# A spectral filter with a feed-forward gate on one core: the transform over d handed on from chunk to chunk, two numbers of its planner, and one accumulating load asked for a step sooner

## The chip, the cores and the metric

The kernel runs on one core of a Trainium2 chip. A core has a matrix engine (TensorE, PE in the profile), a vector engine (VectorE, DVE), a scalar engine (ScalarE, ACT), GpSimd (POOL) and SyncE (SP), which here only issues DMAs. PE's weight loads have a row of their own in the profile (PEld). Each engine works through its own queue in order, and engines wait for each other through semaphores. A letter q behind an engine's name (SPq, ACTq) is its sequencer, which issues DMAs.

The metric is the time of one execution on the device in microseconds (us), smaller is better. The kernel before was run three times.

## The reference, cut to what matters

```python
x = A_x                                   # 1 x 2048 x 1024
xn = _layernorm(x, axis=-1)
X = rfft2(xn)                             # over s (2048) and d (1024)
s = irfft2(X * (w_r + 1j * w_i))          # spectral filter
h = silu(xn @ w1)                         # 1024 -> 3584
g = silu(h @ w2)                          # 3584 -> 1024
out = x + s * g
```

So there are two branches on the same normed input: a Fourier filter over both axes, and a feed-forward net whose output gates the filter's. At the end they are multiplied and the input is added.

## The kernel before, in words

**Two matrix products, and everything else between them.** Rows of x are cut in four chunks c of 512 rows, each in four parts p of 128. Fp32 operands are split in two fp16 halves, so that each product is three fp16 matmuls. The first product (`mm1`, lines 457 to 479) walks a list `order` of 112 groups (c, f), one for each chunk and each 128 columns of w1; a group is 24 matmuls (L466). Its silu is taken by ACT (L475) one group later. The second product (`mm2`, lines 545 to 551) is done as seven block products m with eight output tiles j each; a group (m, j) is two times 21 matmuls (L549, L550, L551).

**The planner.** The spectral branch has no place of its own. It is written as Python generators, and the loop over the groups takes steps of them when the program is written. After a group's matmuls come `settle` (the evacuation of the group ahead), `tick` (DMAs that were put off by some groups) and `work` (line 1523). `work` takes one step of the queue `wq` (loading and splitting weights), in seven of eight calls one of `xq` (maxima of the filter and of w2), and then up to three steps of `bg`, in which the spectral branch stands in order. In mm1 that is once a group, in mm2 twice. Whether `bg` may go on is decided by a meter: a callback (line 220) adds up an estimated time for each PE and DVE instruction in `clock["pe"]` and `clock["dve"]`, and `bg` stops while the DVE's clock is more than `LEAD` = 1.0 us ahead of the PE's. The DVE's clock is never let fall more than 1.0 us behind. A step may also yield `PAUSE`, which ends the call; any other yielded value has no effect. An instruction's place in the text so fixes what is queued ahead of it on its engine.

**The transform over d.** `fd_gen(c)` (lines 816 to 915), one generator for each chunk, is the first part of the forward Fourier transform. For part p, `fa_mat(c, p)` (lines 799 to 806) makes 24 matmuls of 128 columns into a PSUM tile `fa`; the tag "ft" has two such tiles. `fa_evac(c, p)` (lines 808 to 814) clears a strip of a tile `L` on POOL (L811) and copies the PSUM tile to it with two ACT instructions (L812, L813). `bfly(p)` (lines 820 to 868) then is DVE work in two steps. The loop of lines 870 to 878 runs over i = 0 to 5: matmuls of part i, evacuation of part i - 1, butterflies of part i - 2. Each pass has at least two yields, also where it has nothing to do. Chunk 0 has its four `fa_mat` and two of its `fa_evac` elsewhere, in the entry of the kernel, and passes 0 and 1 are empty for it.

After the butterflies come four radix-4 steps j (lines 894 to 911): `high_r(j - 1)` on ACT (L884, L886), two DVE instructions, `low_r(j - 1)` (L889, L890), `radix4` on DVE, and a sum `total[j]` (L909, tile `vt`). Line 910 then takes 0.8 us off the DVE's clock. After the four, `high_r(3)` and `low_r(3)` end the chunk.

**What follows in bg.** When the four chunks are through and `w2max_gen` is done, the memory of the forward part is closed, and `f_gen` (the transform over s, the filter, the way back) and the four `i_gen` (c in the order 1, 3, 0, 2; lines 1254 to 1453) follow. An `i_gen` makes its matmuls `iu` (L1280 for odd c, L1288 for even c) into the two PSUM tiles of tag "ft"; they are evacuated by ACT (`uc`, L1294) and DVE (`ub`, L1296, L1297). Ahead of them POOL copies an edge into the input tile `zt` (L1249, L1252).

**wmax_gen** (lines 921 to 943), in `xq`, finds the largest filter value: 18 DVE maxima, one more over them (L935), a reduction over the partitions on POOL (L937), and then on DVE a power of two of that (`pow2`, L230, and lines 940 to 942). One yield stands between POOL's instruction and `pow2`.

**w2_gen** (lines 411 to 453), in `wq`, makes the operands of mm2. Step n loads raw tile n + 4 on SP's queue (L420, tile `jr`, six buffers), splits tile n on ACT (L257, `w<-jr`) and finishes tile n - 1 on DVE (L260). For the products m = 4 and 5 the operand is a sum of two blocks: `join(n + 2)` (L424) has POOL issue a DMA that adds the second block of w2 to raw tile n + 2.

Of the kernel before, what the change touches and what calls it, by code (L numbers as in the profile page):

```python
# [132 lines left out]
def spectral_ffn(ctx, tc, x, w_r, w_i, w1, w2, ca, kc, ci, tw, pm, out):  # L133
# [29 lines left out]
    def small(name, n=1):  # L163
        return sm.tile([128, n], F32, name=name)
# [51 lines left out]
    clock = {"pe": 0.0, "dve": 0.0}  # L216
# [12 lines left out]
    def pow2(e, m):  # L229
        nc.vector.tensor_single_scalar(e.bitcast(I32), m.bitcast(I32), 0x7F800000, op=OP.bitwise_and)  # L230
        nc.vector.tensor_single_scalar(e, e, 2.0**-100, op=OP.max)

    def radix4(sign, b, d, o):

        sub = nc.vector.tensor_tensor
        plus, minus = ((2, 7), (6, 3)) if sign < 0 else ((6, 3), (2, 7))

        def pick(i):
            st = i[1] - i[0]
            stop = i[1] + (1 if st > 0 else -1)  # L240
            return o[:, i[0]:stop:st]

        sw = d[:, 1, ::-1]
        sub(o[:, 0:2], b[:, 0], b[:, 1], op=OP.add)
        sub(o[:, 4:6], b[:, 0], b[:, 1], op=OP.subtract)
        sub(pick(plus), d[:, 0], sw, op=OP.add)
        sub(pick(minus), d[:, 0], sw, op=OP.subtract)
# [8 lines left out]
    def high(hi, raw, scale):  # L256
        nc.scalar.activation(hi, raw, AF.Copy, scale=scale)  # L257

    def low(lo, raw, scale, hi):
        nc.vector.scalar_tensor_tensor(lo, raw, scale, hi, op0=OP.mult, op1=OP.subtract)  # L260
# [146 lines left out]
    def w2_block(m, q, b):  # L407
        r, h = W2_BLOCKS[m][b]
        return w2[(2 * q + r) * 128:(2 * q + r + 1) * 128, h * 512:(h + 1) * 512]

    def w2_gen():

        todo = [(m, q) for m in range(7) for q in range(NP)]
        raw = {}

        def load(n):
            if n < len(todo):
                m, q = todo[n]
                raw[n] = J["p"].tile([128, 512], F32, name=f"jr{n}", tag="jr", bufs=6)
                nc.sync.dma_start(raw[n], ws[m][q] if m in ws else w2_block(m, q, 0))  # L420

        def join(n):
            if n < len(todo) and todo[n][0] in SUMMED:
                nc.gpsimd.dma_start(raw[n], w2_block(*todo[n], 1), accum_op=OP.add)  # L424

        def split(n):
            m, q = todo[n]
            if q % 7 == 0:
                w2t[m, q // 7] = fp.tile([128, 7, 2, 512], F16, name=f"w2_{m}_{q // 7}", tag="big", bufs=4)
            high(w2t[m, q // 7][:, q % 7, 0], raw[n], sc2[:, q:q + 1])  # L430

        def rest(n):
            m, q = todo[n]
            w = w2t[m, q // 7][:, q % 7]
            low(w[:, 1], raw.pop(n), sc2[:, q:q + 1], w[:, 0])
            ready2[0] = n

        for n in range(4):
            load(n)
        yield 0  # L440
        yield 0
        for n, (m, q) in enumerate(todo):
            while q % 7 == 0 and (done2[0] < m - 1 or chunks[0] <= (3 if m else q // 7) and m < 2):
                if n and ready2[0] < n - 1:
                    rest(n - 1)
                yield 0
            load(n + 4)
            join(n + 2)
            split(n)
            if n and ready2[0] < n - 1:  # L450
                rest(n - 1)
            yield 0.1
        rest(n)
# [345 lines left out]
    def fa_mat(c, p):  # L799
        ps = pt.tile([128, 8, 128], F32, name=f"fa{c}_{p}", tag="ft")  # L800
        sl, xt = slice(p * 128, (p + 1) * 128), xnT[c]
        for d in range(8):
            nc.tensor.matmul(ps[:, d], xt[:, 0, d, sl], A["ca"][:, 0, d], start=True, stop=False)
            nc.tensor.matmul(ps[:, d], xt[:, 0, d, sl], A["ca"][:, 1, d], start=False, stop=False)
            nc.tensor.matmul(ps[:, d], xt[:, 1, d, sl], A["ca"][:, 0, d], start=False, stop=True)
        psa[c, p] = ps

    def fa_evac(c, p):
        ps = psa.pop((c, p))
        t0 = A["p"].tile([128, 8, 2, 65], F32, name=f"L0_{c}_{p}", tag="L0", bufs=2)  # L810
        nc.gpsimd.memset(t0[:, :, 1, 0:1], 0.0)  # L811
        nc.scalar.activation(t0[:, :, 0], ps[:, :, 0:65], AF.Copy)  # L812
        nc.scalar.activation(t0[:, :, 1, 1:64], ps[:, :, 65:128], AF.Copy)  # L813
        l0[c, p] = t0

    def fd_gen(c):
# [50 lines left out]
            stt(rv(1, 7), up(qq[:, 3]), -RH, up(pp[:, 3]), op0=OP.mult, op1=OP.subtract)  # L867
            tt(v[:, 1, 0:1], ee[:, 0, 0, 0:1], ee[:, 1, 0, 0:1], op=OP.subtract)

        for i in range(6):  # L870
            if i < 4 and c:
                fa_mat(c, i)
            if 1 <= i <= 4 and (c or i > 2):
                fa_evac(c, i - 1)
            yield 0
            if i >= 2:
                yield from bfly(i - 2)
            yield 0
        o, sp, total, both = {}, {}, {}, {}

        def high_r(j):
            room = ap.tile([128, 2048 + 256 * len(THREE)], F16, name=f"Rs{c}_{j}", tag="Rs", bufs=2)
            both[j] = room[:, 2048:].rearrange("p (q h k) -> p q h k", h=2, k=128)
            nc.scalar.activation(both[j][:, :, 0], total[j], AF.Copy, scale=2.0**-21)  # L884
            sp[j] = room[:, 0:2048].rearrange("p (q h k) -> p q h k", h=2, k=256)
            nc.scalar.activation(sp[j][:, :, 0], o[j], AF.Copy, scale=2.0**-21)  # L886

        def low_r(j):
            nc.vector.scalar_tensor_tensor(sp[j][:, :, 1], o[j], 2.0**-21, sp[j][:, :, 0], op0=OP.mult, op1=OP.subtract)  # L889
            nc.vector.scalar_tensor_tensor(both[j][:, :, 1], total[j], 2.0**-21, both[j][:, :, 0], op0=OP.mult, op1=OP.subtract)  # L890
            defer(2, lambda: nc.sync.dma_start(vd[j][:, :, c], sp[j]))
            defer(2, lambda: nc.sync.dma_start(vs[j][:, :, c], both[j]))

        for j in range(4):
            sl = slice(128 * j, 128 * j + 128)
            if j:
                high_r(j - 1)
            b = ap.tile([128, 2, 2, 128], F32, name=f"Rb{c}_{j}", tag="Rb", bufs=1)
            d = ap.tile([128, 2, 2, 128], F32, name=f"Rd{c}_{j}", tag="Rd", bufs=1)
            nc.vector.tensor_tensor(b, vt[:, 0:2, :, sl], vt[:, 2:4, :, sl], op=OP.add)  # L900
            nc.vector.tensor_tensor(d, vt[:, 0:2, :, sl], vt[:, 2:4, :, sl], op=OP.subtract)
            if j:
                low_r(j - 1)
            r = ap.tile([128, 8, 128], F32, name=f"Ro{c}_{j}", tag="Ro", bufs=1)
            radix4(-1, b, d, r)
            o[j] = r.rearrange("a (q r) k -> a q (r k)", r=2)
            total[j] = ap.tile([128, len(THREE), 128], F32, name=f"vt{c}_{j}", tag="E", bufs=1)
            some = o[j][:, THREE[0]:THREE[-1] + 1]
            nc.vector.tensor_tensor(total[j], some[:, :, 0:128], some[:, :, 128:256], op=OP.add)  # L909
            clock["dve"] -= 0.8  # L910
            yield 3.9
        high_r(3)
        yield 0.5
# [7 lines left out]
    def wmax_gen():  # L921

        ap = A["p"]
        mt = small("mw", 18)
        tl = {}
        for k in range(21):
            if k < 18:
                src = (w_r, w_i)[k % 2].rearrange("(p r) k -> p (r k)", p=128)
                tl[k] = ap.tile([128, 912], F32, name=f"wm{k}", tag="x", bufs=4)
                nc.sync.dma_start(tl[k], src[:, 912 * (k // 2):912 * (k // 2) + 912])  # L930
            if k >= 3:
                nc.vector.tensor_reduce(mt[:, k - 3:k - 2], tl.pop(k - 3), axis=AX.X, op=OP.max, apply_absolute_value=True)
            yield 1.1
        m = small("mwx")
        nc.vector.tensor_reduce(m, mt, axis=AX.X, op=OP.max)  # L935
        mm = small("mwm")
        nc.gpsimd.partition_all_reduce(mm, m, 128, bass.bass_isa.ReduceOp.max)  # L937
        yield 0.3
        pow2(e_w, mm)
        nc.vector.reciprocal(zs, e_w)  # L940
        nc.vector.tensor_single_scalar(zs, zs, 2.0**-26, op=OP.mult)
        nc.vector.tensor_single_scalar(s_sc, e_w, 2.0**-21, op=OP.mult)
        yield 0.3
# [551 lines left out]
    with tc.manual_schedule():  # L1495
# [73 lines left out]
        for c in range(4):  # L1569
            add(bg, fd_gen(c))  # L1570
# [17 lines left out]
        for n, (c, f) in enumerate(order):  # L1588
# [3 lines left out]
            if ln[3].done and n >= 22 and not f_job:  # L1592
                add(xq, wmax_gen())
                max_job = add(xq, w2max_gen())
                f_job = add(bg, switch(A, open_f, 1, max_job))
                add(bg, f_gen())
                add(bg, switch(B, open_i, 6, lag=2))
                for k in IORDER:
                    add(bg, i_gen(k))
# [111 lines left out]
```

## Time and profile before

| | us |
|---|---|
| three runs, median (lowest to highest) | 1236.11 (1231.04 to 1239.41) |
| the profiled execution, own time | 1234.66 |
| its span, first to last instruction | 1232.9 |
| PE busy in the span | 1215.5 (99%) |
| DVE, ACT, POOL busy | 1003.9, 495.3, 133.1 |
| first matmul of mm2 starts at | 640.6 |

The span is what the trace covers; the execution's own time is 1.8 us longer. In the views a row gives the start, the duration, the engine, the line of the kernel, what is written and read (`out<-in`, without buffer numbers), the shape, and in square brackets how long the engine stood idle just before and what ended that (`<-`). Matmuls are pipelined: one of 512 columns lasts 0.38 us in its row, but the next begins 0.22 us after it.

### The profile page before, as it was taken

To read this page: it belongs to the slowest core of one execution; us is meant where nothing else is said; L and a number is where in the kernel's file an instruction comes from. 1 tells how busy PE (TensorE), PEld (TensorE's weight loads), DVE (VectorE), ACT (ScalarE), POOL (GpSimd) and SP (SyncE) were. 2 spreads that over 40 slices of the span, in tenths; PEclk is the share of its full clock that TensorE was granted. 3 is DMA by queue.
4 is the path that set the end of the run, shared out by engine and by line. 5 is a ranking of instruction groups with operands and counts; after the bars stand their busy time and mean duration, and the time that the engine had idled before them with its cause. 6 is when DMAs were issued, how large, how long until landed. Compare 5 with 4: busy or idle time off the path is not lost.

```text
span 1232.9 us, 19149 instructions
## 1 busy us (share of the span) xinstructions
PE 1215.5 (99%) x6992; PEld 616.5 (50%) x6992; DVE 1003.9 (81%) x2006; ACT 495.3 (40%) x670; POOL 133.1 (11%) x256
## 2 busy tenths in 40 slices
PE   8999999999999999999999999999999999999998
PEld 5544445444444444445445555544545554455545
DVE  7778997896998798869967989895377876997766
ACT  6675553355475554343534222221122222333212
POOL 3320100001000000001110121142111111000000
PEclk9999999999999999999999999999999999999999
DMA  8887686736878977588998999987979999897677
GB/s 250 185 199 180 171 247 191 211 116 196 264 251 269 316 236 223 158 244 186 198 288 273 260 254 233 310 248 225 289 207 313 259 333 313 293 351 242 229 239 281
DMA packets 285055, 299.98 MB, mean 243 GB/s; under 512 B 48928, under 2 KB 211744, under 8 KB 284576
## 3 DMA queue, kind: packets, MB, share of 16 engines
q1 hardware_dynamic: 264944, 239.95, 66.8%
q10 hardware_dynamic: 15840, 50.67, 11.8%
q0 software_dynamic: 4176, 8.13, 3.6%
q8 instruction: 55, 0.90, 0.3%
q14 instruction: 40, 0.33, 0.1%
HBM read 188.05 MB, written 104.35 MB: 237 GB/s over the span
## 4 chain that ended last, share of the span: by engine, by line
PE 70%; DVE 9%; DMA 9%; ACT 3%; issue 2%; SPq 0%; POOL 0%; ACTq 0%; DVEq 0%; POOLq 0%
PE pa L466 33%; PE pb L549 10%; PE pb L551 10%; PE pb L550 10%; DMA ht<-hd_dif 3%; PE id L1370 2%; DMA jr<-in_B_w_dram 2%; DMA zd<-zq 1%; ACT xp L750 1%; PE iu L1280 1%; PE fx L1000 1%; DMA vq<-vd 1%; DVE w L260 1%; DMA pl<-pd 1%; PE iu L1288 1%
## 5 line engine op out<-in xcount | busy, mean ns | idle before, releaser
L466 PE MATMUL pa<-xnT,w 128*128 128x512 f16 x2688 | 584.5, 379 | 1.2 <-ACT w L257 0.7
L466 PEld LDWEIGHTS <-w 128*128 128x128 f16 x2688 | 261.2, 98 | 312.2 <-issue 1.2
L549 PE MATMUL pb<-w,ht 128*128 128x512 f16 (+2 forms) x812 | 301.8, 373 | 0.0
L551 PE MATMUL pb<-w,ht 128*128 128x512 f16 (+2 forms) x812 | 301.6, 373 | 0.0
L550 PE MATMUL pb<-w,ht 128*128 128x512 f16 (+2 forms) x812 | 301.4, 373 | 0.0
L551 PEld LDWEIGHTS <-ht 128*128 128x128 f16 x812 | 79.7, 98 | 91.9 <-issue 1.6
L549 PEld LDWEIGHTS <-ht 128*128 128x128 f16 x812 | 79.9, 98 | 87.6 <-issue 1.1
L550 PEld LDWEIGHTS <-ht 128*128 128x128 f16 x812 | 79.8, 98 | 87.6 <-issue 1.4
L257 ACT ACTIVATE w<-jr,sc 128x512 f16<-128x512 f32 x98 | 68.7, 714 | 89.3 <-DMA jr<-in_B_w_dram 41.9
L475 ACT ACTIVATE h<-pa,s 128x512 f32<-128x512 f32 x112 | 75.3, 676 | 66.3 <-PE pa L466 50.7
L260 DVE SCALAR_TENSOR_TENSOR w<-jr,sc,w 128x512 f16<-128x512 f32 x98 | 71.5, 745 | 14.4 <-ACT w L257 14.3
L260 DVE SCALAR_TENSOR_TENSOR hoone<-h,hs,hoone 128x2048 f16<-128x2048 f32 x28 | 65.6, 2344 | 9.9 <-ACT hoone L257 9.9
L257 ACT ACTIVATE hosum<-hr,hs 128x1536 f16<-128x1536 f32 x28 | 44.0, 1572 | 71.1 <-DVE hr L505 38.7
L257 ACT ACTIVATE hoone<-h,hs 128x2048 f16<-128x2048 f32 x28 | 55.9, 1995 | 38.4 <-DVE h L509 19.9
L260 DVE SCALAR_TENSOR_TENSOR hosum<-hr,hs,hosum 128x1536 f16<-128x1536 f32 x28 | 50.7, 1812 | 1.8 <-ACT hosum L257 1.8
L257 ACT ACTIVATE w<-w1r,rs 128x1024 f16<-128x1024 f32 x28 | 31.9, 1143 | 44.2 <-DVE w L260 31.4
L504 DVE TENSOR_TENSOR hr<-h 128x1024 f32<-128x1024 f32 x28 | 34.4, 1228 | 17.3 <-ACT h L475 17.3
L642 ACT ACTIVATE pl<-pl,c 128x512 f32<-128x512 f32 (+2 forms) x28 | 17.7, 657 | 70.1 <-DVE pl L618 42.7
L424 POOL DMA_DIRECT2D jr<-in_B_w_dram x28 | 24.8, 1009 | 178.7 <-DMA jr<-in_B_w_dram 92.7
L1032 ACT ACTIVATE zq<-Z,zs 128x1024 f16<-128x1024 f32 x16 | 18.4, 1147 | 55.3 <-DVE Z L1123 25.9
L1123 POOL TENSOR_TENSOR Z<-yb 128x32 f32<-128x32 f32 x32 | 18.4, 594 | 182.8 <-DVE yb L1102 182.8
L260 DVE SCALAR_TENSOR_TENSOR w<-w1r,rs,w 128x1024 f16<-128x1024 f32 x28 | 35.6, 1274 | 2.3 <-ACT w L257 2.2
(239 smaller groups left out, 1565.6 us busy)
## 6 DMA issues: line engine op xcount, KB each, us to landing
w1r<-in_B_w_dram SPq DMA_DIRECT2D x28, 512.0 KB, 6.5
hd_sum<-hosum SPq DMA_DIRECT2D x56, 256.0 KB, 2.9
hd_one<-hoone SPq DMA_DIRECT2D x56, 256.0 KB, 3.8
hd_dif<-hoone SPq DMA_DIRECT2D x56, 256.0 KB, 3.9
w2m<-in_B_w_dram SPq DMA_DIRECT2D x28, 512.0 KB, 5.9
ht<-hd_dif ACTq DMA_DIRECT2D x32, 448.0 KB, 9.6
jr<-in_B_w_dram SPq DMA_DIRECT2D x56, 256.0 KB, 6.7
ht<-hd_sum ACTq DMA_DIRECT2D x32, 448.0 KB, 5.7
```

What stands on the lines that cost most here:

```text
L257: nc.scalar.activation(hi, raw, AF.Copy, scale=scale)
L260: nc.vector.scalar_tensor_tensor(lo, raw, scale, hi, op0=OP.mult, op1=OP.subtract)
L424: nc.gpsimd.dma_start(raw[n], w2_block(*todo[n], 1), accum_op=OP.add)
L466: nc.tensor.matmul(ps, w[:, wh, d], xt[:, xh, d], start=(n == 0), stop=(n == 23))
L475: nc.scalar.activation(hq[:, 2 * (c % 2) + f % 2], ps, AF.Silu, scale=s1[:, f:f + 1])
L504: tt(sums[:, 0:2], hq[:, 0::2], hq[:, 1::2], op=OP.subtract)
L549: nc.tensor.matmul(ps, hh[:, 0], w[:, 0], start=first, stop=False)
L550: nc.tensor.matmul(ps, hh[:, 0], w[:, 1], start=False, stop=False)
L551: nc.tensor.matmul(ps, hh[:, 1], w[:, 0], start=False, stop=last)
L1032: nc.scalar.activation(zqs[q][:, 0, :, 16 * j:16 * j + 16], zs_[u], AF.Copy, scale=zs)
L1123: eng.tensor_tensor(Z[:, ns, pos], x0[:, :, ls], x1[:, :, ls], op=o_)
L1370: nc.tensor.matmul(ps[:, g, cols], us[g][:, uh, 4 * r + p], C["ci"][:, ch, g, r, cols], start=(r == 0 and n == 0), stop=(r == 1 and n == 2 ...
```

## The change

There are four edits. (1) The loop over i starts at 2 in every chunk: it keeps the evacuations of parts 2 and 3 and the butterflies. The four `fa_mat` of chunk c + 1 and the first two `fa_evac` move into the radix-4 steps of chunk c: at j = 0 and 1 one `fa_mat` each, at j = 2 and 3 the evacuation of part j - 2 and right behind it `fa_mat` of part j. They stand ahead of `high_r(j - 1)` in the step. (2) The 0.8 us are no longer taken off the DVE's clock. (3) Three yields instead of one stand between POOL's reduction in `wmax_gen` and `pow2`. (4) `join` is called for tile n + 3 in step n.

```diff
             load(n + 4)
-            join(n + 2)
+            join(n + 3)
             split(n)
...
-        for i in range(6):
-            if i < 4 and c:
-                fa_mat(c, i)
-            if 1 <= i <= 4 and (c or i > 2):
+        for i in range(2, 6):
+            if 2 < i < 5:
                 fa_evac(c, i - 1)
             yield 0
-            if i >= 2:
-                yield from bfly(i - 2)
+            yield from bfly(i - 2)
             yield 0
...
         for j in range(4):
+            if c < 3:
+                if j < 2:
+                    fa_mat(c + 1, j)
+                else:
+                    fa_evac(c + 1, j - 2)
+                    fa_mat(c + 1, j)
             sl = slice(128 * j, 128 * j + 128)
             if j:
                 high_r(j - 1)
...
             nc.vector.tensor_tensor(total[j], some[:, :, 0:128], some[:, :, 128:256], op=OP.add)
-            clock["dve"] -= 0.8
             yield 3.9
...
         nc.gpsimd.partition_all_reduce(mm, m, 128, bass.bass_isa.ReduceOp.max)
-        yield 0.3
+        for _ in range(3):
+            yield 0
         pow2(e_w, mm)
```

## The prediction

> **What bounds the kernel now.** I read the page's head, the busy time by stage, and then who PE waited for.
>
> ```profile
> span 1232.9 us, 19149 instructions
> PE 1215.5 (99%) x6992; PEld 616.5 (50%) x6992; DVE 1003.9 (81%) x2006; ACT 495.3 (40%) x670; POOL 133.1 (11%) x256
> L466 PE MATMUL pa<-xnT,w 128*128 128x512 f16 x2688 | 584.5, 379 | 1.2 <-ACT w L257 0.7
> ```
> ```profile
> 0.00:25.00 25.00, 20.83 (x150) 15.29 (x151) 18.75 (x33) 14.10 (x15) 7.08 (x25) 1.00 0.94 297
> 25.00:641.00 616.00, 611.07 (x3228) 294.44 (x3227) 524.83 (x1019) 322.55 (x387) 56.52 (x104) 1.00 0.76 214
> 641.00:1228.00 587.00, 583.48 (x3617) 306.79 (x3615) 458.48 (x949) 157.98 (x268) 69.50 (x128) 0.99 0.89 273
> 1228.00:1233.00 5.00, 0.17 (x3) 0.00 (x0) 1.89 (x7) 0.69 (x2) 0.00 (x0) 0.84 0.18 54
> ```
> ```profile
> PE fa L803 <- ACT L L813: 4.3, 2, 2.8
> PE iu L1288 <- DVE ub L1297: 2.4, 1, 2.4
> PE eps L1160 <- POOL edge L1153: 1.0, 1, 1.0
> ```
>
> The second view has the stage, its length, and busy PE, PEld, DVE, ACT, POOL. PE is the bound. Outside the first 25 us and the last 5, which the change doesn't touch, it is idle 4.9 us in mm1's stage and 3.5 us in mm2's. The edits neither add nor remove a matmul, so all that can be won is these waits and what hangs on them, and the time can only come out much different by new waits of PE. A group of mm1 is 24 x 584.5 / 2688 = 5.2 us.
>
> **Edit 1: the old waits of `fa`.** Two of the twelve `fa_mat` of chunks 1 to 3 waited:
>
> ```profile
> 305.40 0.22 PE L803 MATMUL fa<-cas,xnT 128*128 128x128 f16 x1 [1.54 <-ACT L L813]
> 417.38 0.22 PE L803 MATMUL fa<-cas,xnT 128*128 128x128 f16 x1 [2.79 <-ACT L L813]
> ```
>
> Both are part 2 of a chunk: it needs the PSUM tile of part 0, and ACT came late to evacuate it. For the first, DVE had stood behind POOL's reduction of `wmax_gen`, and ACT behind DVE:
>
> ```profile
> 278.31 0.17 DVE L935 TENSOR_REDUCE mwx<-mw 128x1 f32<-128x18 f32 x1
> ...
> 287.11 0.15 DVE L230 TENSOR_SCALAR e_w<-mwm 128x1 int32<-128x1 int32 x1 [6.37 <-POOL mwm L937]
> 295.40 1.15 ACT L257 ACTIVATE w<-w1r,rs 128x1024 f16<-128x1024 f32 x1 [14.12 <-DVE w L260]
> ```
>
> Both waits lie at a chunk's start, where no `fa_mat` stands any more: 1.54 + 2.79 = 4.3 us go.
>
> **Edit 1: the new waits.** At j = 2 and 3 the evacuation and the `fa_mat` that needs its tile are now in one step. PE gets to that `fa_mat` at the end of the group behind which the step stands; ACT gets to the evacuation when it is through with what was queued before. The place where the evacuation will stand is where `high_r(j - 1)` begins now. At j = 2 of chunks 0, 1 and 2:
>
> ```profile
> 153.15 0.42 ACT L884 ACTIVATE Rs<-vt 128x256 f16<-128x256 f32 x1 [1.74 <-DVE vt L909]
> ```
> ```profile
> 269.27 0.42 ACT L884 ACTIVATE Rs<-vt 128x256 f16<-128x256 f32 x1 [2.28 <-DVE vt L909]
> ```
> ```profile
> 380.75 1.06 ACT L283 ACTIVATE junk<-w1r 128x1024 fp8e4<-128x1024 f32 x1 [9.57 <-DMA w1r<-in_B_w_dram]
> 387.24 0.40 ACT L884 ACTIVATE Rs<-vt 128x256 f16<-128x256 f32 x1
> ```
> ```profile
> L813 ACT ACTIVATE L<-fa x16: 578/586/612, 23.0 to 454.3; 128x504 f32<-128x504 f32 x16
> ```
>
> ```profile
> 135.12 25.92 PE pa L466 x120
> ...
> 207.90 31.08 PE pa L466 x144
> ...
> 354.89 20.76 PE pa L466 x96
> ```
>
> The last fence is from the chain of work: stretches of whole groups. Counting ACT's silus, one a group, the three steps stand behind the groups that end at 135.12 + 4 x 5.18 = 155.8, 207.90 + 12 x 5.18 = 270.1 and 354.89 + 5 x 5.19 = 380.8. In the first two ACT is free at 153.15 - 1.74 = 151.4 and 269.27 - 2.28 = 267.0; with L813 and its like, L812, 0.59 each less 0.1 of overlap, the tile is free at 152.5 and 268.1: 3.3 and 2.0 us ahead of PE. At j = 3 of these chunks I expect no wait either. In chunk 2 it would be 388.3 against 380.8, 7.5 us late, because ACT had stood 9.57 us for a load of w1.
>
> But the step comes sooner than that. The empty passes take 16 steps out (4 in each chunk), at most three to a group: 16 / 3 = 5.3 groups. Edit 2 makes DVE's clock 16 x 0.8 = 12.8 us dearer, 2.5 groups. So the last chunk ends some 3 groups, about 15 us, sooner; counted forward group by group by the planner's rule, j = 2 and 3 of chunk 2 fall behind the groups that end at 354.9 and 365.3. There ACT does this:
>
> ```profile
> 357.27 1.58 ACT L257 ACTIVATE hosum<-hr,hs 128x1536 f16<-128x1536 f32 x1 [5.33 <-DVE hr L505]
> 365.31 1.15 ACT L257 ACTIVATE w<-w1r,rs 128x1024 f16<-128x1024 f32 x1 [1.35 <-PE pa L466]
> 366.36 1.04 ACT L390 ACTIVATE junk<-w2m 128x1024 fp8e4<-128x1024 f32 x1
> 367.31 0.19 ACT L390 ACTIVATION_READ_ACCUMULATOR junk<-w2m 128x1 f32 x1
> ```
>
> At 354.9 ACT is idle, no wait. At 365.3 it has just begun a weight half, which waited for that very group of PE, and a maximum; the evacuation would begin at 367.4 and end at 368.5. PE waits 3.2 us. I take 3 us for all six places; the ends are 0 and 7.5 + 3.2 = 10.7 (late at j = 2 as in the order of now, and at j = 3 as just read).
>
> Moved with `fa_evac`: POOL's clearing of `L` (L811), whose buffer has long been read, at nothing: POOL is 11% busy. No DMA moves. On ACT the evacuations now stand ahead of `high_r`, 1.1 us each; DVE waits for `high_r` but is not on the path.
>
> **Edit 2** issues nothing. The sum itself (L909) takes 425 ns, so the meter was short by 0.4 us a step rather than long; DVE's queue is a little shorter in the radix steps. Nothing on the path; what it moves is counted above.
>
> **Edit 3.** DVE's 6.37 us wait goes or shrinks: two more groups are 10.4 us, and POOL's result was there 287.11 - 278.31 = 8.8 us after DVE's last maximum began. PE sees none of it directly; its one effect was the wait at 305.40, counted already. `w2max_gen` ends two calls later, well before `bg` asks for it. Value 0.
>
> **Edit 4.** POOL can't issue the adding DMA before the load that it adds to has landed, whatever the step:
>
> ```profile
>   DMA jr<-in_B_w_dram: 92.7, 8
> DMA to landing us min/median/max: 4.0/7.7/11.7
> ```
> ```profile
> 1020.39 8.42 DMA jr<-in_B_w_dram
> 1029.37 10.56 DMA jr<-in_B_w_dram
> ```
>
> The first fence is of L424: what POOL waited for there, and the joins' own time to land. In the second, from the chain of work, a load lands at 1028.8 and its join begins at 1029.4. A join that waits for its load is no sooner on the chip for standing a step sooner in the text. Value 0 for ACT's wait. Queued behind a join on POOL is the edge copy that `iu` needs; bounds 0 and the 7.7 us of a rival below.
>
> **The wait of `iu`.**
>
> ```profile
> 1039.96 0.72 ACT L257 ACTIVATE w<-jr,sc 128x512 f16<-128x512 f32 x1 [11.04 <-DMA jr<-in_B_w_dram]
> 1040.59 0.58 ACT L1294 ACTIVATE uc<-iu 128x512 f32<-128x512 f32 x1
> ```
> ```profile
> 1042.54 1.82 PE L1288 MATMUL iu<-kk,zt 128*128 128x129 f16 x24 [2.44 <-DVE ub L1297]
> 1044.15 0.63 PE L549 MATMUL pb<-w,ht 128*128 128x512 f16 x1
> ...
> 1047.11 0.38 PE L550 MATMUL pb<-w,ht 128*128 128x512 f16 x1
> ```
>
> ACT stands 11 us for a joined tile, with `uc` behind it, and PE behind that. Behind `iu` seven matmuls take 1047.11 - 1044.15 = 2.96 us, where 7 x 0.217 = 1.52 would do: 1.4 us more, 3.8 in all. Edit 4 doesn't cure it, but the shift does: `bg` is some 15 us sooner against the loads, whose places in `wq` stay, so this `iu` is asked for before ACT gets to that tile. I take 3.8 us as gone, and 1.5 us for a new meeting of that kind (ends 0 and 7.7).
>
> Behind the gap of 2.79 us at 417.38 mm1 ran on at 15.54 / 72 = 0.22 us a matmul:
>
> ```profile
> 418.88 15.54 PE pa L466 x72
> ```
>
> [...]
>
> **The sum.** -4.3 + 3 - 3.8 + 1.5 = -3.6 us on the profiled execution's 1234.66: 1231.1. The median of the runs, 1236.11, stands 1.45 us above it, so I say 1232.5 for the median.
>
> **Rivals.**
>
> *A, slower: `fa_mat` waits for ACT in its own step.* If the steps of chunk 2 fall behind ACT's load wait (380.75) as they do now, PE waits 7.5 + 3.2 us: 1236.1 - 4.3 + 10.7 = 1242.5, the wait of `iu` staying. For it: the evacuation has lost its lead of two steps. Against it: ACT is idle at j = 2 in all three rows that I expect. It decides when the six waits exceed 4.3 + 3.8 = 8.1 us together.
>
> *B, nothing is gained: the waits only move.* The wait of `iu` finds another place, and the new `fa` waits take most of the old ones: -4.3 + 3 = -1.3, 1234.8. For it: 7.7 us is the middle of a join's time to land, and ACT splits the 28 joined tiles in order whatever `bg` does.
>
> *C, the edge copy is late.*
>
> ```profile
> 880.64 0.93 POOL L1249 COPY zt<-zps 128x16 f16<-128x16 f16 x1
> ```
> ```profile
> 882.98 2.68 PE iu L1280 x48
> ```
>
> The copy waited behind joins, and ended 1.4 us before the first `iu`. If `iu` comes one group of mm2 (42 x 0.217 = 9.1 us) sooner and the loads do not, PE waits 9.1 - 1.4 = 7.7 us: 1232.5 - 1.5 + 7.7 = 1238.7. Against it: `zt`'s loads, ahead of the joins' on SP, move along with `bg`.
>
> *D, all is gained:* no new wait, 1236.1 - 8.1 = 1228.0.
>
> That `bg` ends sooner is worth nothing by itself: its last butterfly is over some 54 us before the span's end.
>
> ```profile
> L1417 DVE SCALAR_TENSOR_TENSOR rows<-sk,spa x4: 284/284/285, 1161.0 to 1178.5; 128x128 f32<-128x128 f32 x4
> ```
>
> **The numbers.** Forecast (about 1229 to 1234) 0.42, B (1234 to 1237) 0.2, A 0.13, C 0.1, D 0.1, something unseen 0.05. Range 1226 to 1242: from D to A and C, with room for the runs' own spread of 8 us; the forecast's own range is 1229 to 1236. About 1% is what a measurement of this kernel can tell from no change, 12.4 us: faster by over that would need more than all of PE's waits outside the ends (4.9 + 3.5 us, and 1.4 of slow matmuls), 0.03; slower by over it needs A and C at once or a wait unseen, 0.05; within it 0.92.
>
> **What would show it.** No wait at the first `fa_mat` of a chunk's start; `fa` before the butterflies; one wait of about 3 us at part 3 of chunk 3, none at the other five places. L230 without idle time ahead of it. Joins still starting as their loads land, with ACT's waits for `jr` as long as before. No `iu` wait at the third matmul group of c = 0. The forecast is wrong if PE's idle time for `fa` is over 6 us, if `iu` of c = 1 waits for the copy, or if PE idles at `fx` or `id`, where it did not.

## The result and the profile after

The changed kernel takes 1239.41 us (median of 22 runs, lowest 1235.8), the kernel before 1235.21 (22 runs, 1231.0 to 1240.38): ratio 1.0033, 95% interval [1.0018, 1.0047]. The forecast was 1232.5, so the sign was wrong, and the time lies inside the range. Two runs were disturbed and are left out of the ratios: one of the changed kernel (5003.72 us) and the profiled one of e10_spread_join below (1593.52 us), which therefore has no profile here. The profiled execution took 1236.4 us, its span 1234.5; it is the second fastest of the 22, so a second profile (e0_after, span 1239.1) stands beside it below.

Busy time by stage of the changed kernel; columns as in the prediction (length; busy PE, PEld, DVE, ACT, POOL; granted clock):

```profile
25.00:644.50 619.50, 612.10 (x3226) 295.59 (x3225) 530.42 (x1035) 324.47 (x387) 54.71 (x105) 1.00 0.76 214
644.50:1229.50 585.00, 582.36 (x3618) 306.41 (x3616) 452.01 (x932) 156.84 (x269) 68.81 (x127) 1.00 0.89 273
```

PE is idle for 7.4 us in mm1's stage, where it was 4.9, and for 2.6 in mm2's, where it was 3.5. The first matmul of mm2 starts at 644.58, where it was 640.59. So in this execution the loss is in mm1: 4.0 us there, and 2.4 less from there to the end. Who PE waited for (line, waited for, us in total, times, longest):

```profile
PE fa L803 <- ACT L L813: 6.7, 2, 5.4
...
PE eps L1163 <- POOL edge L1156: 2.0, 1, 2.0
...
PE fx L996 <- DVE xd L1067: 0.5, 1, 0.5
```

No wait of `iu` is left (the dots leave out the start of the kernel). The two waits of `fa`, by the timeline, and the last matmul of the second one's part:

```profile
154.80 0.22 PE L803 MATMUL fa<-cas,xnT 128*128 128x128 f16 x1 [1.29 <-ACT L L813]
...
374.64 0.26 PE L803 MATMUL fa<-cas,xnT 128*128 128x128 f16 x1 [5.45 <-ACT L L813]
...
377.05 0.31 PE L805 MATMUL fa<-cas,xnT 128*128 128x128 f16 x1
```

Neither is where a wait was before. The first is part 2 of chunk 1 (j = 2 of chunk 0), the second part 3 of chunk 3 (j = 3 of chunk 2). After the second the 24 matmuls take 377.05 + 0.1 - 374.64 = 2.5 us, where 24 x 0.056 = 1.3 us does at 154.80 (their starts there stand 0.056 us apart, and 0.105 us here): 1.2 us more. What ACT did ahead of the first (one row) and the second, and DVE ahead of the second:

```profile
149.97 1.15 ACT L257 ACTIVATE w<-w1r,rs 128x1024 f16<-128x1024 f32 x1 [3.06 <-DVE w L260]
...
367.35 2.00 ACT L257 ACTIVATE hoone<-h,hs 128x2048 f16<-128x2048 f32 x1 [2.24 <-issue]
...
371.43 1.15 ACT L257 ACTIVATE w<-w1r,rs 128x1024 f16<-128x1024 f32 x1 [1.50 <-DVE w L260]
372.48 1.04 ACT L390 ACTIVATE junk<-w2m 128x1024 fp8e4<-128x1024 f32 x1
...
373.52 0.59 ACT L812 ACTIVATE L<-fa 128x520 f32<-128x520 f32 x1
374.01 0.58 ACT L813 ACTIVATE L<-fa 128x504 f32<-128x504 f32 x1
```
```profile
368.39 1.81 DVE L260 SCALAR_TENSOR_TENSOR hosum<-hr,hs,hosum 128x1536 f16<-128x1536 f32 x1
370.12 1.28 DVE L260 SCALAR_TENSOR_TENSOR w<-w1r,rs,w 128x1024 f16<-128x1024 f32 x1
```

The prediction let the copy follow a weight half that begins at 365.3. Here ACT stands 1.50 us for DVE's half of a weight tile, which stands behind DVE's `hosum`, and gets to that half only at 371.43. The copy ends at 374.6, where 368.5 was expected, and PE came for it at 369.2 (374.64 - 5.45), where 365.3 was expected. The same thing stood ahead of both waits of the kernel before: ACT's halves of weight tiles at 295.40 and at 414.17 had stood 14.12 and 2.14 us for DVE, and behind the second PE waited 2.79 us although the copy then stood a pass of the loop ahead of the matmuls.

The second profile of the same kernel has the same two waits of `fa`, and a larger one of `eps`:

```profile
PE fa L803 <- ACT L L813: 6.8, 2, 5.3
PE eps L1163 <- POOL edge L1156: 3.1, 1, 3.1
...
PE pb L549 <- DMA ht<-hd_dif: 1.0, 1, 1.0
```

The stretch behind `eps` in it, against before (length, busy PE, granted clock):

```profile
810.00:815.00 5.00, 5.00 (x19) 0.50 1.02 121
```
```profile
810.00:815.00 5.00, 5.00 (x23) 0.66 0.97 221
```

The first is of the changed kernel's second profile, the second of before. In both TensorE's clock drops behind the wait of `eps`, in before too, where that wait is 1.0 us. The clock's drop belongs to what a wait costs. The second profile's span is 4.6 us longer than the first's (1239.1 and 1234.5). Its first matmul of mm2 starts 0.9 us later (645.50), so 3.7 us of this lie behind it, where `eps` and `ht` wait 2.1 us longer.

### The profile page after: what moved, and what is told of

The parts are those of the page before. It is cut to its first block, busy times and chain, and to the rows that moved or that the text cites. A ratio compares the mean times of both kernels' runs of the same rounds, so it can differ in the third digit from the quotient of the medians.

```text
span 1234.5 us, 19142 instructions
## 1 busy us (share of the span) xinstructions
PE 1215.2 (98%) x6992; PEld 617.2 (50%) x6992; DVE 1003.1 (81%) x2006; ACT 496.1 (40%) x670; POOL 130.6 (11%) x256
## 4 chain that ended last, share of the span: by engine, by line
PE 70%; DVE 10%; DMA 9%; ACT 3%; issue 2%; SPq 1%; POOL 0%; ACTq 0%; DVEq 0%; POOLq 0%
PE pa L466 34%; PE pb L549 10%; PE pb L551 10%; PE pb L550 10%; PE id L1373 2%; DMA ht<-hd_dif 2%; DMA jr<-ws 1%; DMA zd<-zq 1%; DMA vs<-vs 1%; ACT xp L750 1%; DMA wq<-in_A_w_i_dram 1%; PE iu L1291 1%; PE iu L1283 1%; DMA ht<-hd_sum_d 1%; DVE w L260 1%
## 5 line engine op out<-in xcount | busy, mean ns | idle before, releaser
L260 DVE SCALAR_TENSOR_TENSOR hoone<-h,hs,hoone 128x2048 f16<-128x2048 f32 x28 | 65.6, 2341 | 13.7 <-ACT hoone L257 13.7
```

## The experiments

Two theories. *Own wait*: the copy and the matmuls that need it now stand in one step, and PE waits there for ACT; the prediction sized this at 3 us, it is 6.7 plus 1.2 for slow matmuls, and that is the loss. *Place* (the rival): edits 1 and 2 move all later steps of the background by a few groups; they meet PE, ACT, POOL and the DMAs in other combinations, and the loss is that, whatever the moved steps do. Ratios are to the kernel before on the same chip, with a 95% interval.

### Each edit alone, and all but one

**e2_move_only**: edit 1 alone (the front's diff of the transform over d, without the line of the meter).

> Edit 1 alone; the 0.8 us are taken off as before, one yield in wmax_gen, join as before. Theory (same-step waits): PE waits 5 us or more at fa at j = 2 and 3, more than in the changed kernel, because DVE is let run further behind; slower than before by 3 to 8 us. Rival (edits 2 to 4 cost the time): within 2 us of before or faster.

Measured: 1248.31 us, 1.0098 [1.0076, 1.012].

```profile
PE fa L803 <- ACT L L813: 11.8, 3, 5.9
...
PE fx L1003 <- DMA vq<-vd: 3.2, 1, 3.2
PE fx L1003 <- issue: 2.2, 1, 2.2
```

Alone it costs three times what all four edits cost together: 11.8 us of its own waits, and 5.4 us of `fx`, where neither the kernel before nor the change has more than 0.5. The steps behind the transform stood 3 to 17 us sooner, two of them some 40 (by the starts of the sixteen `yb` of mm2's steps), so I read the `fx` waits as steps that came ahead of their loads; one of the two ended with a load (`vq`), what ended the other the profile doesn't show.

**e5_meter_only**: edit 2 alone, a line that issues nothing.

```diff
-            clock["dve"] -= 0.8
```

> Edit 2 alone (the 0.8 us that the last steps of the transform over d took off the meter are no longer taken off), all else as before. It issues no instruction. Theory of place: the steps behind the transform come about as late as with edits 2, 3 and 4 together, where the sixteen steps of mm2's stage stood 10 to 18 us later; they meet other waits at mm2 (fx or eps or iu, together some 10 us where before has 6), and the time is 1240 to 1243. Rival (edit 3 made that loss, the meter is worth nothing): no step stands more than 3 us off, 1235 to 1236.

Measured: 1249.51 us, 1.0122 [1.0091, 1.0153]. No wait of `fa` at all, and instead:

```profile
PE fx L999 <- DMA wq<-in_A_w_i_dram: 6.3, 1, 6.3
PE fx L992 <- ACT zq L1031: 4.3, 1, 4.3
PE eps L1159 <- POOL edge L1152: 3.5, 1, 3.5
PE iu L1279 <- DMA jr<-in_B_w_dram: 3.2, 1, 3.2
```

The sixteen steps of mm2's stage stood 19 to 60 us later, most about 20. This line issues no work and costs 15 us, more than either theory was said to give: place has a price, and a large one.

**e6_wmax_only**: edit 3 alone.

```diff
-        yield 0.3
+        for _ in range(3):
+            yield 0
```

> Edit 3 alone (the scale chain waits two empty steps for the maximum over the partitions), all else as before. The VectorE wait of 6.4 us at L230 goes; no step that PE waits for is meant to move by more than 1 to 2 us. Both theories: within 2 us of before, 1233 to 1237; a larger move, either way, would say that this edit too shifts the steps behind it.

Measured: 1229.73 us, 0.9957 [0.994, 0.9974], faster than both kernels; outside what either theory was said to give. The idle time of DVE ahead of L230 in it, and PE's waits:

```profile
  POOL mwm L937: 0.6, 1
```
```profile
PE fa L803 <- ACT L L813: 1.6, 1, 1.6
PE iu L1289 <- DVE ub L1298: 1.4, 1, 1.4
```

DVE's 6.37 us at L230 became 0.6. The wait of `fa` at 305.40 (1.54 us) is gone, that at 417.38 fell from 2.79 to 1.6, and that of `iu` from 2.44 to 1.4 with no slow matmuls behind it (1.4 us): 1.5 + 1.2 + 1.0 + 1.4 = 5.1 us, and the span is 5.4 us shorter. This edit moves places too: the sixteen steps of mm2's stage stand 2 to 6 us off, one of them 30 us later. Why the two later waits shrank was not taken apart.

**e4_join_only**: edit 4 alone.

```diff
-            join(n + 2)
+            join(n + 3)
```

> Edit 4 alone. Theory: a join starts when its load has landed whatever the step, so ACT's wait for the joined tile ahead of the third iu of c = 0 (11 us) and PE's 2.4 us stay, and the time is that of before within 1.5 us. Rival (an earlier join lands earlier): that wait shrinks by one step, up to 4.5 us, PE's wait goes, and the kernel is 3 to 4 us faster.

Measured: 1234.44 us, 0.9988 [0.9969, 1.0007], not told from before.

```profile
PE iu L1280 <- POOL zt L1249: 3.7, 1, 3.7
...
PE iu L1288 <- DVE ub L1297: 0.3, 1, 0.3
```

`iu` now waits for the edge copy (rival C's wait, at half the price worked out, though here it is not `iu` that comes sooner). The later `iu` wait fell from 2.4 to 0.3, but ACT's half of that joined tile stands where it stood, at 1039.96 before:

```profile
1040.11 0.72 ACT L257 ACTIVATE w<-jr,sc 128x512 f16<-128x512 f32 x1 [10.34 <-DMA pd<-pl]
```

PE only comes later, after the 3.7 us. One wait paid for the other.

**e3_no_move**: edits 2, 3 and 4 without 1.

> Edits 2, 3 and 4 without edit 1. Theory: no new wait at fa; the first old one (1.54 us) goes with DVE's wait for the reduction; within 3 us of before, rather faster. Rival (the meter or the waits set apart cost it): slower than before by 3 us or more.

Measured: 1243.03 us, 1.0062 [1.0038, 1.0086].

```profile
PE fx L993 <- ACT zq L1032: 4.2, 1, 4.2
PE eps L1160 <- POOL edge L1153: 2.7, 1, 2.7
PE iu L1288 <- DVE ub L1297: 2.6, 1, 2.6
PE iu L1280 <- POOL zt L1249: 2.2, 1, 2.2
```

No `fa` wait, and mm2's steps 10 to 18 us later, two of them 40 and 50. Edit 1 added to this makes it some 3.6 us faster by the medians: it brings its own waits, and in the change the steps stand 0 to 10 us sooner than before instead of later. Counted in PE's matmuls, the `fx`, `eps` and `iu` of e3 stand exactly where e5 has them, and yet it is 0.6% faster by the ratios: with edits 3 and 4 in, e5's waits for `wq` and `jr` (6.3 and 3.2 us) don't come. So place alone doesn't fix the price.

**e14_no_join**: the changed kernel without edit 4.

> The changed kernel without edit 4 (edits 1, 2 and 3). If edit 4 is what sets eps later (the second half of a join's split stands on VectorE ahead of the step that eps waits for, 0.75 us), eps falls from 2.0 to 3.1 us to 1.0 to 1.5, and the fa waits stay at 1.5 and 5.4: 1236 to 1238. If edit 4 does nothing there: eps as before and 1238 to 1240; if it was a cure, an iu wait of 2 to 3 us comes back at 1030 to 1045 and 1240 to 1243.

Measured: 1239.18 us, 1.0034 [1.0017, 1.0051], as with it, and `eps` waits 3.1 us: my guess that a join's second half on DVE sets `eps` back fell. Within the change edit 4 is worth nothing.

### The moved steps' own wait, with places left as they fall

**e1_spread**: the changed kernel with no copy in the step of the matmuls that need it.

```diff
-                if j < 2:
-                    fa_mat(c + 1, j)
+                if j == 0:
+                    fa_mat(c + 1, 0)
+                    fa_mat(c + 1, 1)
+                elif j == 1:
+                    fa_evac(c + 1, 0)
+                elif j == 2:
+                    fa_mat(c + 1, 2)
+                    fa_evac(c + 1, 1)
                 else:
-                    fa_evac(c + 1, j - 2)
-                    fa_mat(c + 1, j)
+                    fa_mat(c + 1, 3)
```

> The changed kernel with one thing moved: at j = 0 parts 0 and 1 are multiplied, at j = 1 part 0 is evacuated, at j = 2 part 2 is multiplied and part 1 evacuated, at j = 3 part 3 is multiplied, so that no matmul stands in the step that evacuates its PSUM tile. Theory (PE waits for ACT because evacuation and matmul share a step): the 6.7 us of idle time at fa fall below 1 us and the half-speed matmuls behind them go, so the span falls by 7 to 9 us from 1234.5, to about 1226 to 1228, and the kernel is faster than before by 4 to 7 us. Rival (the loss comes from the steps of bg standing sooner, against other loads): fa no longer waits, but the time stays within 2 us of the changed kernel's, with waits elsewhere.

Measured: 1238.22 us, 1.0029 [1.0011, 1.0048].

```profile
PE eps L1168 <- POOL edge L1161: 4.1, 1, 4.1
PE pa L466 <- DVE e L292: 3.2, 1, 3.2
```

All waits of `fa` are gone, and the time hardly moved; `fx` waits 1.8 us and `ht` 2.3 us besides. *Own wait* as the whole cause falls here.

**e16_copy_sooner**: the cleanest form of that test, only the two copies one step sooner.

```diff
-                if j < 2:
-                    fa_mat(c + 1, j)
-                else:
-                    fa_evac(c + 1, j - 2)
-                    fa_mat(c + 1, j)
+                fa_mat(c + 1, j)
+                if 1 <= j <= 2:
+                    fa_evac(c + 1, j - 1)
```

> The changed kernel with one thing moved: each of the two copies (fa_evac of parts 0 and 1) stands one step sooner, at j = 1 and 2, behind that step's matmuls. The matmuls of each step, the steps and their prices are those of the change, so the later steps stand where they stand in it. Theory (the copy in the matmuls' own step is the change's own loss): the fa waits of 1.5 and 5.4 us and the slow matmuls behind the second go to under 1.5 us together, the other waits stay (eps 2 to 3): 1231 to 1235. Rival (place is all): the time goes to other waits (pa, eps, fx, ht), 1237 to 1239, as in e1_spread.

Measured: 1237.45 us, 1.0025 [1.0006, 1.0043].

```profile
PE eps L1161 <- POOL edge L1154: 3.7, 1, 3.7
PE pa L466 <- DVE e L292: 3.1, 1, 3.1
PE pb L549 <- DMA ht<-hd_dif: 2.6, 1, 2.6
```

6.7 us of `fa` went, and 3.1 of `pa`, 2.6 of `ht` and 0.6 to 1.7 more of `eps` came. PE, no longer held up at 374, arrives sooner at steps whose other work is sooner by less or not at all: DVE's `e` (L292) stands 1.85 us sooner than in the change (496.27 and 498.12), and the `Z` on POOL ahead of the edge copies 1.65 us later (804.82 and 803.17). The rival's 1237 to 1239 was right.

**e9_spread_same_steps**, **e10_spread_join**, **e11_own_same_steps**: edit 1 in the kernel before, the two emptied steps of each chunk and the meter kept; spread as in e1 (e9), spread and with edit 4 (e10), in the change's form (e11).

> The moved matmuls and copies of e1_spread (no step with a wait for its own copy) in the kernel before, with every step and its price left as before: the two steps at each chunk's start that held them stay as empty steps, the meter and the waits as before, joins as before. So the work moves and the places of all other steps do not. Theory of place: before's fa waits (4.5 us) go, nothing else changes, eps and iu waits of before stay: 1229 to 1232, ratio 0.994 to 0.998. Rival (the moved work costs by itself, as VectorE then serves PE's other matmuls later): 1235 to 1239.

> e9_spread_same_steps with edit 4 (a join one step later behind its load). Theory of place: as in e4_join_only the iu wait at 1042 shrinks and a wait of iu for the edge copy of 3 to 4 us comes at 883; with the fa waits gone, 1229 to 1232. Rival (moved work costs by itself): 1234 to 1238.

> Edit 1 in its own form (copy and matmuls in one step) in the kernel before, with every step and its price left as before, the two emptied steps of each chunk staying as empty steps; edits 2, 3 and 4 not in. Theory of place: before's two fa waits (4.5 us) go and fa waits of the new form come (6 to 12 us, as in the changed kernel and in e2_move_only), all else as before: 1237 to 1243. Rival (edit 1's loss in e2 came from the shift of the steps behind, not from its own waits): 1232 to 1236.

Measured: 1236.36 us, 1.0013 [0.9999, 1.0027]; 1236.24 us, 1.0019 [1.0001, 1.0036]; 1236.93 us, 1.0018 [1.0003, 1.0034]. The first fence is of e9, the second of e11:

```profile
PE pa L466 <- ACT h L475: 5.3, 3, 1.9
PE s L266 <- ACT h L475: 2.7, 1, 2.7
```
```profile
PE fa L803 <- ACT L L813: 4.8, 2, 4.7
PE pa L466 <- DVE e L292: 3.7, 1, 3.7
```

These didn't do what they were made for: the steps of mm2's stage did not stay, most came 10 to 17 us sooner. The prices of the steps were kept, but the matmuls' own price had moved. My reading of the planner, not tried by itself: PE's clock is counted up with the `fa` matmuls, which gives DVE room; beside empty steps that room was forfeited, beside the radix steps it is used. Seen as they are, e9 and e11 stand in the same places as each other, counted in PE's matmuls: with the own wait (e11, 4.8 us) and without it (e9) the times are 0.6 us apart.

### Place

**e8_before_late**: the kernel before with two empty pauses (one group each) ahead of the background of mm2's stage.

```diff
+        yield PAUSE
+        yield PAUSE
         load_k(0)
         yield PAUSE
```

> The kernel before with two empty pauses of one group each ahead of the first step of the mm2 stage's background and nothing else: all of that stage's steps some 10 us later, no instruction more or less. Theory of place: the time moves by a few us with no change of the work, because mm2's matmuls meet other steps: 1238 to 1243, as with edits 2 to 4 together, with an iu, fx or eps wait of 2 to 4 us that before hasn't. Rival (place is worth nothing, the edits' own work counts): 1235 to 1236.

Measured: 1239.43 us, 1.0044 [1.0022, 1.0066], with the same work. The steps stand 3 to 17 us later, one of them 34. Its profiled execution (1233.02) is the fastest of its 12 and shows only `eps` at 1.7 us beside before's waits, so where the usual one lost isn't seen.

**e7_spread_shift**, **e13_spread_shift2**, **e15_after_shift2**, **e17_copy_sooner_shift2**: the same pauses in e1_spread (one in e7, two in e13), in the changed kernel (e15) and in e16 (e17).

> The kernel of e1_spread (moved steps, no step with a wait for its own copy; edits 2, 3, 4 in it) with one thing more: one empty pause of one group ahead of the first step of the mm2 stage's background, so that these steps stand about where they stood before (e1 had them 1 to 8 us sooner). Theory of place: the fa waits stay gone (4.5 us less than before), eps, fx and ht waits go back to before's sizes, a wait of iu for the edge copy may stay as in e4_join_only (3 to 4 us): 1232 to 1235. Rival (the moved matmuls and copies cost by themselves, wherever the rest stands): 1237 to 1239 again.

> e1_spread with two empty pauses ahead of the mm2 stage's first background step (e1 had none: 1238.2; e7 one: 1236.4). No fa wait; the pa wait for VectorE of 3.3 us at 497 stays, as it lies ahead of the pauses. Theory of place: only what mm2 meets changes, 1233 to 1240, the sign not foretold. It stands beside e15_after_shift2, which has the same pauses and the moved steps in the form of the change.

> The changed kernel with two empty pauses ahead of the mm2 stage's first background step. fa waits stay at 1.5 and 5.4 us with 1 to 2 us of slow matmuls behind them, as they lie ahead of the pauses; eps, fx, ht and iu change. If the fa waits are the change's own loss, the time is 2 to 5 us over that of e13_spread_shift2 (no fa wait, a pa wait of 3.3 us with 1.7 us of slow matmuls in its stead, so rather 2 than 5). If the place of mm2's steps is all, both are within 1 us of one another.

> e16_copy_sooner with the two empty pauses of e13 and e15 ahead of the mm2 stage's first background step. If both parts of the loss are what they seem (own waits some 5 us by e13 against e15, place some 4 us by e15 against the change), 1227 to 1231, as e13_spread_shift2; if the place of e13 was chance of its own, 1232 to 1237.

| form of the moved steps | no pause | one | two pauses |
|---|---|---|---|
| as changed | 1239.41, 1.0033 [1.0018, 1.0047] | not run | e15: 1234.68, 0.9997 [0.9978, 1.0015] |
| copies a step sooner | e16: 1237.45, 1.0025 [1.0006, 1.0043] | not run | e17: 1230.94, 0.9975 [0.9954, 0.9996] |
| spread | e1: 1238.22, 1.0029 [1.0011, 1.0048] | e7: 1236.44, 1.0021 [1.0002, 1.004] | e13: 1228.52, 0.9955 [0.9938, 0.9972] |

The medians of a row or column were measured on different chips or at different times, so the ratios stand beside them. e13 came out under the 1233 to 1240 expected of it, e15 6.2 us above e13 where 2 to 5 were expected, and e7 between what its two theories gave. PE's waits in e15, e13 and e17, in this order (the profiled execution of e15, 1237.65 us, is above its median, that of e17, 1224.51, the fastest of ten):

```profile
PE fa L803 <- ACT L L813: 7.5, 2, 6.1
...
PE eps L1165 <- POOL edge L1158: 2.2, 1, 2.2
```
```profile
PE pa L466 <- DVE e L292: 3.1, 1, 3.1
...
PE eps L1170 <- POOL edge L1163: 0.5, 1, 0.5
```
```profile
PE pa L466 <- DVE e L292: 1.5, 1, 1.5
```

Both causes are there. Across: the pauses alone win 4.7 us in the changed kernel, 6.5 in e16, 9.7 in e1 (0.36, 0.50 and 0.74% by the ratios). Down: curing the moved steps' wait wins 1 to 2 us without pauses, and 3.7 to 6.2 with them (0.04 to 0.08% and 0.22 to 0.42%). The first pair lies within the intervals, and so does the copies' 0.22%; that of e13 against e15, 0.42%, doesn't. That the two cures bring more together than singly is thus seen in the spread form, by little more than the intervals, and is not told for the copies. Within a column the places are the same: counted by the matmuls of mm1 and mm2 that PE begins ahead of it, every `fx`, `eps` and `iu` of the change, e16 and e1 stands behind the same number, and so does every one of e15, e17 and e13 (the last `fx` behind 3339 and 3360; before has 3381). So what is read down a column isn't place. Without pauses the time that `fa` no longer waits for is spent at `pa`, `ht` and `eps`; with them mm2's stage has almost no waits, and most of the win is kept. Why just two pauses in this place free `eps` isn't settled: the edge copies stand on POOL behind `Z`, which waits for DVE (18.46 us for `yb` at 803.17 in the change, 19.06 at 804.82 in e16), but what set DVE back there wasn't taken away by itself.

**e12_wmax_join**: edits 3 and 4, the two that lost nothing alone.

> Edits 3 and 4 together, without 1 and 2 (the two edits that were not slower alone: 1229.7 and 1234.4 against 1234.5 and 1235.5). Both theories place it under both kernels. Theory of place: e6's fa wait of 1.6 us stays, its iu wait of 1.4 us at 1038 goes, and the iu wait for the edge copy at 883 that came with edit 4 alone (3.7 us) comes: 1229 to 1233. Rival (gains of single edits add up): 1228 to 1229.

Measured: 1231.3 us, 0.9973 [0.9957, 0.9988]. Not better than edit 3 alone, on another chip (0.9957); no gain is seen from adding edit 4. The best two are e13 and e6, both under the kernel before and the changed one, and not told apart.

**e0_after**: the changed kernel again, for the second profile shown above.

> The changed kernel again, for a second profile beside the first. Waits that come from the order of the work stand at the same places within 1 us (fa 1.5 and 5.5 us, eps 2); what differs between the two profiles is chance of one run. 1238 to 1240.

Measured: 1239.2 us, 1.0045 [1.0026, 1.0064].

## Why the prediction was wrong, step by step

- *Old waits of `fa`, -4.3*: right. No `fa_mat` waits at a chunk's start, and the first of a chunk stands ahead of the butterflies.
- *New waits of `fa`, taken as +3*: the term that failed. The place (part 3 of chunk 3) and the mechanism were right; its wait is 5.4 us for the 3.2 worked out, 1.2 us of slow matmuls weren't counted, and part 2 of chunk 1, given as free by 3.3 us, waits 1.3: 6.7 + 1.2 = 7.9. The step read ACT's place for the copy from rows of the kernel before. In the change ACT stands ahead of the copy for DVE's half of a weight tile (1.50 us at 371.43, and 3.06 us ahead of the first), and DVE is never idle by as much as 0.1 us from 343.1 us until that half: a radix step (361.57 to 366.1), work of mm1 and of w2, and `hosum` stand ahead of it. That it is the radix step that makes the half late is read from this order; it was not taken away by itself.
- *The wait of `iu`, -3.8*: right; the shift removed it.
- *New meetings, +1.5*: in the first profile right (`eps` +1.0, `fx` +0.5), in the second too small (`eps` +2.1, `ht` +1.0, and 0.50 of the clock behind `eps` where before has 0.66).
- The sum with what was measured: -4.3 + 7.9 - 3.8 + 1.5 = +1.3, and the first profile's span is 1.6 longer. The medians differ by 4.2; the second profile (1240.91 us, above the median) has the rest and more, as `eps`, `ht` and the clock behind them.
- *Edit 2, nothing on the path*: it issues nothing, but what it moves isn't small: alone it costs 15 us, and edit 1 alone 13, where all four together cost 4. Their shifts have opposite signs (19 to 60 us later, 3 to 43 sooner), and the prediction priced neither. The change without edit 2 was not run, so what it is worth there stays open.
- *Edit 3, value 0*: wrong for the edit alone, which wins 0.43%: the wait at 305.40 that was named goes with it, and so do parts of two later waits. In the change edit 1 removes the first of these anyway, and the change without edit 3 was not run.
- *Edit 4, value 0*: right (e4 and e14), with rival C's wait of 3.7 us when it stands alone.
- *Rivals*: A's wait decided (`fa_mat` for ACT in its own step), but not for A's reason: ACT's wait for a load of w1 at j = 2 of chunk 2 didn't meet it. It was to decide from 8.1 us on; 6.7 of waits and 1.2 of slow matmuls were measured, and the new meetings made up the rest. B's title, that the waits only move, describes e16 and e1 better than any sum here. C was seen in e4 and e3, not in the change.
- The forecast's own signs against it, `fa` over 6 us and idle time at `fx`, both came (6.7 and 0.5). That the time lay in the range was no merit of the sum: its forecast pointed the other way.

## What to carry to other kernels

When a planner places steps by priced clocks, price a moved step by the queue that will stand at its new place, with the other moved work in it, and not by the rows that stand there now. Where the bound engine is 98% busy and meets many short waits, curing one wait gave back here only what the next ones left, so judge a cure together with a shift of the steps behind it (here empty pauses: in the spread form some 1 us of gain became some 6). An edit that issues no instruction can be the dearest one, if it moves everything behind it.

## What the runs showed of the hardware

One wait can cost more than its own length. The same wait of `pa` for DVE of 3.1 us stands in e13 and in e16; the four us behind it, first e13, then e16 (busy PE, granted clock):

```profile
496.00:500.00 4.00, 3.76 (x18) 1.00 1.01 350
```
```profile
496.00:500.00 4.00, 3.53 (x9) 0.57 1.00 344
```

Nine matmuls were begun in the one where eighteen were in the other. The records of the granted clock show one thing in which the two differ. In the kernel before, stretches at half clock begin at 811.55, 1043.66 and 1231.39 us, and the first two last 3.413 us each; from start to start it is 68 and 55 times that. In the changed kernel they begin at 374.00, 807.50 and 1234.16 us, 127 and 125 times 3.413 us apart. Cut along such steps, the wait fills most of one step in e16 (first view) and is split over two in e13 (second view):

```profile
493.00:496.41 3.41, 0.42 (x2) 1.00 0.97 287
```
```profile
491.21:494.62 3.41, 1.94 (x9) 1.00 0.98 305
494.62:498.04 3.42, 1.80 (x9) 1.00 1.00 329
```

The kernel before and the changed one, cut along their own steps, show the same: with the wait of `iu` the step from 1040.24 us has 1.12 us of busy PE (before), with the second wait of `fa` that from 370.59 has 0.00 (changed), and the step behind each is at half clock. Before's wait of 2.79 us is split over steps with 2.41 and 1.64 us of busy PE (from 412.19 and 415.60), and the clock stays 1.00. Steps with `eps` differ: 2.66 us of busy PE in before (from 808.14), 2.01 in the changed kernel (from 804.08), and half clock behind both. That the place of a wait on the steps decides is read from these cases; it was not tried by itself. Where the steps fall differs between executions of one kernel: the two profiles of the changed kernel have half clock from 374.00 and from 372.51 us, and behind `eps` for one step (3.41 us) and for two. So, by this reading, chance has a part in what a wait costs.

Behind `eps` the clock drops even for a wait of 0.5 us (e13), where nine matmuls of 24 and 8 columns follow the wait:

```profile
805.00:810.00 5.00, 5.00 (x17) 0.66 0.79 289
```

In e17, where `eps` doesn't wait, the granted clock stays 1.00 there (800 to 815 us).

The clock bears on the spread of the runs as well: of 29 runs of the kernel before on one chip the fastest took 1227.97 us at a mean granted clock of 1.000 and the slowest 1241.62 at 0.994. The clock itself makes up about half of these 13.7 us, by an estimate from these figures (0.006 x 1241.62 = 7.4 us). That the place of the steps in each run makes this spread was not tried by itself.
